# The output projection's pairs and the next pair's attention: from a scheduler's order to one written list of steps

## The chip, the cores and the metric

One Trainium2 chip; the kernel runs on one NeuronCore. Its engines work beside each other, each through its own instructions in order: TensorE (PE: matmuls into PSUM banks of 128 x 512 fp32), VectorE (DVE), ScalarE (ACT), GpSimd (POOL) and SyncE (SP), which issues the DMAs. The metric is device time in microseconds (us) of one execution, the median over runs.

## The reference

Two branches read the layer-normalized `x` (2048 x 1024); the result is `x + s * silu(B)`.

```python
qkv = x @ wqkv                       # 32 heads of 32
phi(p) = concat(softmax(p @ w_phi), softmax(-p @ w_phi))
kv = einsum("bhsf,bhsd->bhfd", phi_k, v);  z = einsum("bhsf->bhf", phi_k)
o  = einsum("bhqf,bhfd->bhqd", phi_q, kv) / (einsum("bhqf,bhf->bhq", phi_q, z)[..., None] + 1e-6)
s  = o.reshape(B, S, D) @ wo
B  = (sigmoid(x @ w_gate) * (x @ w_up)) @ w_down      # F = 3584
out = x + s * silu(B)
```

## The kernel before, in words

Every large product is in fp32 accuracy by splitting: an operand `b` becomes `hi` (rounded by ScalarE, L129) and `lo = b - hi` (VectorE, L130), and `mm3` (L132) makes three matmuls hi·hi, hi·lo, lo·hi (L134 to L136). Every large product is also one level of Strassen's scheme (Winograd's form): of a 2 x 2 blocking seven products, B11, T2, T3, B21, T1, T4, B22 (the numbers 0 to 6), instead of eight, with sums of blocks before and of products behind.

The stages follow each other: projections of q, k, v for the first and the second half of the tokens, the gated GLU for both, the down projection, and last the output projection. The change is in the last one alone, from `NTP = TT // 2` on (L636): the 2048 tokens are 8 pairs of tiles of 128 tokens (`u` = 0, 1), and for every pair the kernel makes the attention's output `o` as operands and multiplies them with `wo`. The weights `wo` lie split in SBUF (`WO`, read by `wo_prep`).

The attention of one pair, `attend(tp_)` (L709), has for each half of the columns (`hb` = 0, 1) two kinds of task:

- `phi_transpose(tp_, u, hb, q)` (L657): four 128 x 128 transposes by TensorE (L662) of the normalized features `e` of tile `u` into one of two PSUM banks (`tpr`), and a split of that bank into `phu` (L129, L130). `e` lies in slot 47 + u and comes from DRAM by `e_load(u)` (L651, 512 KB); after the second task of a tile (`q` = 1) the next `e_load` into the same slot is issued (L668).
- `numerator(tp_, hb, q)` (L671): for `b` = 0, 1 four matmuls of 128 x 256 (L680) into one of two banks (`nmr`); ScalarE copies half the partitions to `oraw` (L684) and VectorE adds the others (L685). Behind the second of a half, `o_operands` (L692) makes Strassen's sums of `oraw` on GpSimd (L697, L700, L701, L705) and splits each of the seven operands into slots of `ofr`.

The output projection of pair `tp_` (L1194 on) runs over the seven products `i` in order 0 to 6; each is four `mm3` over `k`, into a bank of `amm`: B11, T2, T3 and T1 open a bank of their own, B21, T4 and B22 continue those of B11, T3 and T1. Behind each product stands its evacuation: B11 by ScalarE (L1210), T2, T3 and the others by VectorE (L1212, L1214, L1221, L1224), then for the four result blocks a multiplication with the gate `g` and an addition of `x` (L1225, L1226), on GpSimd, or in the last pair for T4 and B22 on VectorE; then the store of the block to `out` (L1227) and `gx_load`, which reads `g` and `x` of the block after the next (L1188, L1189). Between the products' steps the loop takes the 12 tasks of `attend(tp_ + 1)` (L1206): task n when `(13 - len(nxt)) * 3 <= 2 * n`, so the next pair's attention lies between this pair's products. The first pair's attention runs inside the down projection.

What decides the order on each engine: the source is recorded, and the scheduling layer (`schedule_with_timeline_sim=True`, L1254) orders each engine's instructions by its own simulated times. In the built program TensorE runs a middle pair's products as B11, T1, B21, T3, T2, T4, B22, not as the source has them. An exception is the kernel's first stage: a list of named single steps, `FIRST` (L752), that the context manager `in_order` (L906) fixes on PE, DVE, ACT, SP and POOL by chaining every instruction to the one before it on its engine. `queued` holds the last instruction of each.

Of the kernel before, what the change touches and what calls it, by code (L numbers as in the profile page):

```python
# [10 lines left out]
F32 = mybir.dt.float32  # L11
# [7 lines left out]
P = 128  # L19
# [14 lines left out]
class Ring:  # L34
# [3 lines left out]
    def next(self):  # L38
        self.n += 1
        return self.items[(self.n - 1) % len(self.items)]  # L40
# [5 lines left out]
B11, T2, T3, B21, T1, T4, B22 = range(7)  # L46
# [3 lines left out]
def hedgehog_glu_kernel(  # L50
# [11 lines left out]
    nc = tc.nc  # L62
# [53 lines left out]
    def halves(*ids):  # L116
        return [slots[i][:, a] for i in ids for a in range(2)]
# [6 lines left out]
    def pair(i):  # L124
        return slots[i][:, 0], slots[i][:, 1]

    def split(o, src):

        nc.scalar.copy(o[0], src)  # L129
        return nc.vector.tensor_sub(o[1], src, o[0].bitcast(F32))  # L130

    def mm3(o, a, b, first, last, **kw):  # L132

        nc.tensor.matmul(o, a[0], b[0], start=first, stop=False, **kw)  # L134
        nc.tensor.matmul(o, a[0], b[1], start=False, stop=False, **kw)  # L135
        nc.tensor.matmul(o, a[1], b[0], start=False, stop=last, **kw)  # L136
# [5 lines left out]
    side = deque()  # L142
# [163 lines left out]
    opening = (B11, T2, T3, T1)  # L306
# [329 lines left out]
    NTP = TT // 2  # L636
# [3 lines left out]
    phu = Ring((44, 20))  # L640
    ofr = Ring((46, 24, 25, 26, 27, 22, 23, 39, 40, 41, 42))
    res = Ring(halves(49, 52))
    gx = Ring(halves(54, 53))
    tpr, nmr, amm = Ring(banks[:2]), Ring(banks[2:4]), Ring(banks[4:])
    e_next, units_ph, of = [0, 0], {}, {}
    oraw = [slots[50], slots[51]]
# [7 lines left out]
            nc.sync.dma_start(whole(47 + u), e_d[2 * tp_ + u, hb])  # L654
        e_next[u] += 1

    def phi_transpose(tp_, u, hb, q):  # L657
        ps = tpr.next()
        e = whole(47 + u)
        for j in range(4):  # L660
            k = 4 * q + j
            nc.tensor.transpose(ps[:, j * P:(j + 1) * P], e[:, k * P:(k + 1) * P], ident)  # L662
# [4 lines left out]
        split((ph[:, 0, :, cs], ph[:, 1, :, cs]), ps.rearrange("p (k t) -> p k t", t=P))  # L667
        if q:  # L668
            e_load(u)

    def numerator(tp_, hb, q):  # L671

        ph = units_ph[hb, q]
        kg = slots[KVB[hb]][:, q].rearrange("p (k m) -> p k m", m=P)
        for b in range(2):
            ps = nmr.next()
            for j in range(2):
                k = 2 * j + b
                for a in range(2):
                    nc.tensor.matmul(ps[:, j * 256:(j + 1) * 256], kg[:, k], ph[:, a, k], start=a == 0, stop=a == 1)  # L680
            hi, lo = [slice(r * 64, r * 64 + 64) for r in (b, 1 - b)]
            o = oraw[hb][hi].rearrange("p u (g t) -> p g u t", t=P)[:, 2 * q:2 * q + 2]
            y, z = [ps[r].rearrange("p (j u t) -> p j u t", j=2, u=2) for r in (hi, lo)]
            nc.scalar.copy(o, z)  # L684
            nc.vector.tensor_add(o, o, y)  # L685
        if q:
            o_operands(tp_, hb)

    def o_operand(tp_, i, b):
        split(pair(of[tp_][i]), b)  # L690

    def o_operands(tp_, hb):  # L692
        (b11, b12), (b21, b22) = [(o[:, 0], o[:, 1]) for o in oraw]
        if hb == 0:
            of[tp_] = {i: ofr.next() for i in range(7)}
            o_operand(tp_, B11, b11)
            nc.gpsimd.tensor_sub(b11, b12, b11)  # L697
            return
        o_operand(tp_, B22, b22)
        nc.gpsimd.tensor_sub(b12, b22, b12)  # L700
        nc.gpsimd.tensor_sub(b22, b22, b11)  # L701
        o_operand(tp_, T2, b22)
        o_operand(tp_, T3, b12)
        o_operand(tp_, B21, b21)
        nc.gpsimd.tensor_sub(b21, b21, b22)  # L705
        o_operand(tp_, T1, b11)
        o_operand(tp_, T4, b21)

    def attend(tp_):  # L709

        out = []
        for hb in range(2):
            tr = {(u, q): (phi_transpose, tp_, u, hb, q) for u in range(2) for q in range(2)}
            nm = [(numerator, tp_, hb, q) for q in range(2)]

            out += [tr[0, 0], tr[0, 1], tr[1, 0], nm[0], tr[1, 1], nm[1]]
        return out
# [185 lines left out]
    queued = {}  # L903
# [218 lines left out]
    for n, (i, j, cs) in enumerate(dsteps):  # L1122
# [32 lines left out]
            side.extend([lambda u=u: e_load(u) for u in range(2)])  # L1155
        if n == ND - NJ:
            step(1000)
            side.extend([lambda fn=fn, a=a: fn(*a) for fn, *a in attend(0)])
# [15 lines left out]

    done = (B21, T1, T4, B22)
    result = [(tp_, i) for tp_ in range(NTP) for i in done]
    gxs = {}
# [5 lines left out]
    def gx_load():  # L1183
        if result:
            tp_, i = result.pop(0)
            t, cols = rows(tp_, i)
            g, xt = gxs[tp_, i] = gx.next(), gx.next()
            nc.sync.dma_start(g, g_d[t, :, cols])  # L1188
            nc.sync.dma_start(xt, x[t * P:(t + 1) * P, cols])  # L1189

    for _ in range(2):
        gx_load()
    abank = {}
    for tp_ in range(NTP):  # L1194
        nxt = attend(tp_ + 1) if tp_ + 1 < NTP else []
        n = 0
        u1, u2, y11, y21 = [res.next() for _ in range(4)]
        for i in range(7):
            if i in opening:
                abank[i] = amm.next()  # L1200
            ps = abank[{B21: B11, T4: T3, B22: T1}.get(i, i)]
            o = [h.rearrange("p (k t) -> p k t", t=P) for h in pair(of[tp_][i])]
            for k in range(4):
                mm3(ps, (o[0][:, k], o[1][:, k]), pair(WO[i][k]), i in opening and k == 0, k == 3, skip_group_check=True)
                n += 1
                while nxt and (13 - len(nxt)) * 3 <= 2 * n:  # L1206
                    fn, *a = nxt.pop(0)
                    fn(*a)
            if i == B11:
                nc.scalar.copy(u1, ps)  # L1210
            elif i == T2:
                nc.vector.tensor_add(u1, u1, ps)  # L1212
            elif i == T3:
                nc.vector.tensor_add(u2, u1, ps)  # L1214
            else:
                g, xt = gxs.pop((tp_, i))
                t, cols = rows(tp_, i)
                eng = nc.vector if tp_ == NTP - 1 and i in (T4, B22) else nc.gpsimd
                if i == B21:
                    y = y11  # L1220
                    nc.vector.tensor_mul(y, g, ps)  # L1221
                else:
                    y = {T1: u2, T4: y21, B22: u1}[i]
                    nc.vector.tensor_add(y, u2 if i == T1 else u1, ps)  # L1224
                    eng.tensor_mul(y, y, g)  # L1225
                eng.tensor_add(y, y, xt)  # L1226
                nc.sync.dma_start(out[t * P:(t + 1) * P, cols], y)  # L1227
                gx_load()


# [27 lines left out]
```

## Time and profile before

| | |
|---|---|
| median of 3 runs | 2415.2 us (2412.53 to 2416.89) |
| the profiled execution | 2410.82 us, span 2409.0 us |
| PE busy | 2370.0 us, 98% |
| DVE, ACT, POOL busy | 1763.4, 1029.4, 960.4 us |
| DMA | 596.29 MB, mean 248 GB/s |
| granted PE clock, mean | 0.998 |

Busy time of PE counts a matmul's whole pipelined length (390 ns for one of 128 x 512, while the next begins about 0.23 us later), so gaps between matmuls are read from starts and from waits, not from the busy share. The "chain" follows the work that ended last back from the end; a "wait" names the instruction that ended an engine's idle time. `bank<-ident,fc` at L662 are the transposes, `bank<-fb,p` and `bank<-x,p` at L680 the numerators; `fc<-e_d` is an `e_load`, `fc<-g_d` and `fc<-x` a `gx_load`, `out<-fc` (or `fb`, `p`) a store.

### The profile page before, as it was taken

The page shows a single profiled execution, that of the slowest core. Times are in us where ns is not written, and L with a number is a line of the kernel's source. Part 1 is how long each engine was busy: PE and PEld are TensorE (multiplying, and loading weights), DVE is VectorE, ACT ScalarE, POOL GpSimd, SP SyncE. Part 2 cuts the span into 40 slices and gives each one's busy share as a digit, 9 for nine tenths or more (in the row PEclk, how much of TensorE's full clock was granted, in tenths as well). Part 3 has the DMA queues.
Part 4 walks back from the last instruction along what each step waited for, and adds up shares of the span by engine and source line. Part 5 has one row for each costly group of instructions (what it writes and reads, how often), then busy time and mean ns, then how long its engine had stood idle before and what let it go on. Part 6 is the DMA issues. An engine that isn't in the chain of part 4 may idle for free.

```text
span 2409.0 us, 31843 instructions
## 1 busy us (share of the span) xinstructions
PE 2370.0 (98%) x10953; PEld 1967.8 (82%) x10953; DVE 1763.4 (73%) x2323; ACT 1029.4 (43%) x1536; POOL 960.4 (40%) x611
## 2 busy tenths in 40 slices
PE   8999999999999999999999999999999999999998
PEld 7888888888888878788888888888888888878776
DVE  8636777767676689658858888646889988866776
ACT  7334344454544433324434444423443334454443
POOL 1332556656565423122434131323334335414554
PEclk9999999999999999999999999999999999999999
DMA  6788977777686787786877666686676766877554
GB/s 248 246 302 318 360 266 256 269 261 271 238 285 237 259 281 257 246 283 220 278 258 267 205 230 208 211 282 230 216 240 228 227 209 228 284 237 253 186 183 134
DMA packets 232291, 596.29 MB, mean 248 GB/s; under 512 B 30528, under 2 KB 30528, under 8 KB 227520
## 3 DMA queue, kind: packets, MB, share of 16 engines
q1 hardware_dynamic: 232128, 594.25, 71.9%
q8 instruction: 86, 1.41, 0.2%
q14 instruction: 77, 0.63, 0.1%
HBM read 359.01 MB, written 235.14 MB: 247 GB/s over the span
## 4 chain that ended last, share of the span: by engine, by line
PE 83%; DVE 8%; DMA 4%; issue 2%; ACT 2%; POOL 0%; SPq 0%; ACTq 0%; DVEq 0%; POOLq 0%
PE bank L134 27%; PE bank L136 26%; PE bank L135 26%; DVE w L130 2%; PE bank L283 1%; DMA fc<-qkv_d 1%; DMA fc<-xo_d 1%; PE bank L484 1%; PE bank L662 1%; PE bank L680 1%; DVE p L130 1%; DVE x L130 1%; DMA fc<-e_d 1%; PE bank L203 0%; ACT x L129 0%
## 5 line engine op out<-in xcount | busy, mean ns | idle before, releaser
L134 PE MATMUL bank<-x,w 128*128 128x512 f32 x2352 | 911.3, 390 | 6.3 <-ACT fb L1036 2.5
L135 PE MATMUL bank<-x,w 128*128 128x512 f32 x2352 | 915.6, 389 | 0.0
L136 PE MATMUL bank<-x,w 128*128 128x512 f32 x2352 | 907.4, 389 | 0.0
L129 ACT CAST w<-fa 128x512 fp32r<-128x512 f32 (+1 forms) x430 | 293.8, 686 | 550.9 <-PE bank L135 364.4
L134 PEld LDWEIGHTS bank<-x,w 128*128 128x128 f32 x2352 | 441.6, 188 | 100.0 <-ACT fb L1036 3.5
L136 PEld LDWEIGHTS bank<-x,w 128*128 128x128 f32 x2352 | 441.6, 188 | 91.9 <-DVE w L130 0.4
L135 PEld LDWEIGHTS bank<-x,w 128*128 128x128 f32 x2352 | 441.7, 188 | 90.2
L130 DVE TENSOR_TENSOR w<-fa,w 128x512 fp32r<-128x512 f32 (+1 forms) x430 | 415.1, 969 | 106.7 <-ACT w L129 99.8
L136 PE MATMUL bank<-w,x 128*128 128x512 f32 x708 | 277.2, 392 | 4.3 <-DVE x L829 4.3
L134 PE MATMUL bank<-w,x 128*128 128x512 f32 x708 | 278.7, 394 | 0.5 <-DVE fc L414 0.5
L135 PE MATMUL bank<-w,x 128*128 128x512 f32 x708 | 277.0, 391 | 0.0
L1046 POOL TENSOR_TENSOR fb<-fb,fc 128x512 f32<-128x512 f32 x57 | 87.9, 1542 | 240.1 <-DVE fc L1045 237.4
L136 PEld LDWEIGHTS bank<-w,x 128*128 128x128 f32 x708 | 133.3, 188 | 33.6 <-DVE x L829 5.4
L134 PEld LDWEIGHTS bank<-w,x 128*128 128x128 f32 x708 | 133.5, 189 | 27.3 <-ACT w L129 0.9
L135 PEld LDWEIGHTS bank<-w,x 128*128 128x128 f32 x708 | 133.5, 189 | 26.6
L619 POOL TENSOR_TENSOR fc<-fc 128x1024 f32<-128x1024 f32 x32 | 81.7, 2554 | 183.4 <-ACT fc L449 128.4
L1045 DVE TENSOR_TENSOR fc<-fc,bank 128x512 f32<-128x512 f32 x84 | 57.3, 682 | 102.7 <-PE bank L136 93.0
L130 DVE TENSOR_TENSOR x<-fa,x 128x512 fp32r<-128x512 f32 x112 | 115.8, 1034 | 20.2 <-ACT x L129 20.1
L129 ACT CAST w<-fb 128x512 fp32r<-128x512 f32 x112 | 69.3, 619 | 130.9 <-PE bank L135 103.9
L130 DVE TENSOR_TENSOR p<-fc,p 128x1024 fp32r<-128x1024 f32 (+2 forms) x97 | 109.2, 1134 | 11.5 <-ACT p L129 9.5
L129 ACT CAST p<-fc 128x1024 fp32r<-128x1024 f32 (+2 forms) x97 | 70.8, 735 | 105.9 <-DVE fc L465 60.5
L130 DVE TENSOR_TENSOR w<-fb,w 128x512 fp32r<-128x512 f32 x112 | 93.5, 835 | 29.8 <-ACT w L129 25.2
(256 smaller groups left out, 3195.9 us busy)
## 6 DMA issues: line engine op xcount, KB each, us to landing
ws_d<-w SPq DMA_DIRECT2D x112, 512.0 KB, 4.1
w<-ws_d SPq DMA_DIRECT2D x112, 512.0 KB, 5.0
fa<-w_gu SPq DMA_DIRECT2D x84, 512.0 KB, 4.3
fa<-h_d SPq DMA_DIRECT2D x84, 512.0 KB, 4.2
fa<-wf_d SPq DMA_DIRECT2D x32, 1024.0 KB, 6.7
h_d<-fc SPq DMA_DIRECT2D x120, 256.0 KB, 3.6
fc<-e_d SPq DMA_DIRECT2D x48, 512.0 KB, 3.9
fc<-qkv_d SPq DMA_DIRECT2D x80, 256.0 KB, 4.5
```

The costliest lines, as they stand in the source:

```text
L129: nc.scalar.copy(o[0], src)
L130: return nc.vector.tensor_sub(o[1], src, o[0].bitcast(F32))
L134: nc.tensor.matmul(o, a[0], b[0], start=first, stop=False, **kw)
L135: nc.tensor.matmul(o, a[0], b[1], start=False, stop=False, **kw)
L136: nc.tensor.matmul(o, a[1], b[0], start=False, stop=last, **kw)
L283: nc.tensor.matmul(ps[:, gs], r[:, gs], bd[:, 4 * f + g], start=True, stop=True)
L484: nc.tensor.matmul(kvb[g // 2][:, g % 2 * 256:g % 2 * 256 + 256], v[:, g].rearrange("p a f -> p (a f)"), ph[:, g].rearrange("p a f -> p (a ...
L619: nc.gpsimd.tensor_mul(ez, e, zb)
L662: nc.tensor.transpose(ps[:, j * P:(j + 1) * P], e[:, k * P:(k + 1) * P], ident)
L680: nc.tensor.matmul(ps[:, j * 256:(j + 1) * 256], kg[:, k], ph[:, a, k], start=a == 0, stop=a == 1)
L1045: v = nc.vector.tensor_add(b, u2 if q == 3 else u1, bank)
L1046: nc.gpsimd.tensor_mul(g, g, b)
```

## The change

The helpers are cut into single steps: `transposes` and `phi_part` (hi, lo) instead of `phi_transpose`; `numerators` and `numerators_out` (cp, ad) instead of `numerator`; `o_sum` and `o_part` instead of `o_operands`; `products`, `product_out`, `scaled` instead of the body of the last loop. `e_load` follows the second pair of transposes of a tile, in whichever order `q` comes. The first pair's attention, inside the down projection, still runs from `attend`, in the old order. Then one list `PAIR` names the steps of a pair's output projection and of the next pair's attention in one sequence; it is run 8 times, in the last without the attention's steps, and `in_order` fixes it on PE, DVE, ACT and POOL (not on SP).

The names: `tr`, `hi`, `lo` and `u hb q`; `nm`, `cp`, `ad` and `hb q b`; `s11`, `sA`, `sB`, `sC` for GpSimd's sums and `x..h`, `x..l` for the splits; `g` with product and `k` for an `mm3`, `v` for an evacuation, `m` and `a` for the multiplication with the gate and the addition of x. In PAIR the products follow as B11, T2, B21, T3, T1, T4, B22: against the built order before, T2 moves from fifth to second and T1 from second to directly ahead of T4. In the last pair B22 is finished in another way: `vB22` makes g·product (VectorE), GpSimd prepares u1·g + x in `last_rest`, and `aB22` adds both.

```diff
-    gx = Ring(halves(54, 53))
-    def phi_transpose(tp_, u, hb, q):
-        ps = tpr.next()
+    def transposes(u, hb, q):
+        tbank[u, hb, q] = ps = tpr.next()
...
+        taken[u] = taken.get(u, 0) + 1
+        if taken[u] % 2 == 0:
+            e_load(u)
+
+    def phi_part(part, u, hb, q):
...
-        if q:
-            e_load(u)
...
-    abank = {}
-    for tp_ in range(NTP):
-        nxt = attend(tp_ + 1) if tp_ + 1 < NTP else []
...
+    PAIR = """
+        tr100 tr000 hi100 gB110 hi000 lo100 gB111 lo000 gB112 tr001 nm001 hi001 tr101 cp001 lo001 gB113 hi101 nm000
+        lo101 gT20 cp000 vB11 gT21 ad000 gT22 ad001 gT23 gB210 tr010 nm010 hi010 tr110 cp010 lo010 nm011 hi110 ad010
+        gB211 cp011 lo110 tr111 ad011 gB212 hi111 tr011 lo111 gB213 hi011 xB11h nm101 lo011 gT30 cp101 xB11l nm100
+        ad101 s11 gT31 cp100 vB21 gT32 ad100 aB21 nm110 vT2 gT33 cp110 nm111 ad110 gT10 cp111 gT11 ad111 gT12 vT3
+        xB22h sA gT13 xB21h xB22l xT1h gT40 vT1 sB xT3h gT41 xB21l gT42 xT3l sC xT2h gT43 gB220 vT4 mT1 xT4h gB221
+        xT1l gB222 xT2l aT1 gB223 vB22 mT4 xT4l aT4 mB22 aB22""".split()
...
+    def scaled(tp_, i, part):
+        u1, u2, y11, y21 = ys[tp_]
+        g, xt = gxs[tp_, i]
+        y = {B21: y11, T1: u2, T4: y21, B22: u1}[i]
+        last = tp_ == NTP - 1 and i == B22
+        eng = nc.vector if tp_ == NTP - 1 and i in (T4, B22) else nc.gpsimd
+        if part == "m":
+            return last or eng.tensor_mul(y, y, g)
+        eng.tensor_add(y, y, y11 if last else xt)
+        t, cols = rows(tp_, i)
+        nc.sync.dma_start(out[t * P:(t + 1) * P, cols], y)
+        gx_load(result.index((tp_, i)) + 2)
+
+    def last_rest():
+        u1, (g, xt) = ys[NTP - 1][0], gxs[NTP - 1, B22]
+        nc.gpsimd.tensor_mul(u1, u1, g)
+        nc.gpsimd.tensor_add(u1, u1, xt)
...
+    queued.clear()
+    with in_order(*[getattr(mybir.EngineType, e) for e in ("PE", "DVE", "Activation", "Pool")]):
+        for tp_ in range(NTP):
+            ys[tp_] = [res.next() for _ in range(4)]
+            if tp_ + 1 < NTP:
+                of[tp_ + 1] = {i: ofr.next() for i in range(7)}
+            for name in PAIR:
+                ahead, f, found = next((ahead, f, m) for form, ahead, f in pair_forms for m in [re.fullmatch(form, name)] if m)
+                if tp_ + 1 < NTP or not ahead:
+                    f(tp_, *found.groups())
+                if tp_ == NTP - 1 and name == "aT1":
+                    last_rest()
```

More of the change, by code (lines that the diff above doesn't have):

```diff
@@ L709, in attend, with o_sum, o_part @@
-    def attend(tp_):
+    def o_sum(which):
+        (b11, b12), (b21, b22) = [(o[:, 0], o[:, 1]) for o in oraw]
+        o, a, b = {"s11": (b11, b12, b11), "sA": (b12, b22, b12), "sB": (b22, b22, b11), "sC": (b21, b21, b22)}[which]
+        nc.gpsimd.tensor_sub(o, a, b)
+    def o_part(tp_, i, part):
+        (b11, b12), (b21, b22) = [(o[:, 0], o[:, 1]) for o in oraw]
+        b = {B11: b11, T1: b11, B22: b22, T2: b22, T3: b12, B21: b21, T4: b21}[i]
+        hi, lo = pair(of[tp_][i])
+        if part == "h":
+            nc.scalar.copy(hi, b)
+        else:
+            nc.vector.tensor_sub(lo, b, hi.bitcast(F32))
@@ L1193, in hedgehog_glu_kernel @@
-    abank = {}
-    for tp_ in range(NTP):
-        nxt = attend(tp_ + 1) if tp_ + 1 < NTP else []
[L1196 to L1228, printed above, removed]
```

125 lines of the change are left out of this document (84 added, 41 removed).

## The prediction

> **What bounds the kernel now.** I read the page first (span, busy shares, chain), then the chain in order of time over one pair of the last stage, then who TensorE waited for there, and then the queues of GpSimd and SyncE.
>
> ```profile
> span 2409.0 us, 31843 instructions
> ...
> PE 83%; DVE 8%; DMA 4%; issue 2%; ACT 2%; POOL 0%; SPq 0%; ACTq 0%; DVEq 0%; POOLq 0%
> ```
>
> The kernel is bound by TensorE. The built programs have the same instructions in the same order on all engines up to 2177.82 us; only what follows can change. The rows below are from the chain (start, length, what), and then TensorE's waits from 2177.8 on (who for whom: us in total, times, longest).
>
> ```profile
> 2281.16 0.70 DVE fb L1212
> ...
> 2284.57 0.23 PE bank L135
> ...
> 2288.58 0.44 PE bank L662 x4
> 2289.02 0.84 PE bank L680 x7
> ...
> 2296.93 0.59 ACT x L129
> 2297.55 0.69 DVE x L130
> ...
> 2299.00 0.70 DVE fb L130
> ...
> 2310.21 0.70 DVE fc L1212
> ```
>
> ```profile
> PE bank L134 <- DVE fb L1214: 3.0, 4, 1.4
> PE bank L134 <- ACT fa L129: 2.8, 1, 2.8
> PE bank L662 <- DVE x L130: 2.5, 4, 0.6
> PE bank L680 <- DVE fb L130: 1.7, 5, 0.3
> PE bank L662 <- DMA fc<-e_d: 1.0, 2, 0.7
> PE bank L134 <- DVE fc L1214: 0.9, 3, 0.3
> ```
>
> The evacuation of T2's product (L1212) comes back after 2310.21 - 2281.16 = 29.05 us: that is one pair. Its TensorE work at the chain's own prices is 84 matmuls of 0.23, eight groups of four transposes at 0.44 and 32 numerator matmuls at 0.12 (0.84 for seven): 19.3 + 3.5 + 3.8 = 26.7 us. So a pair loses some 2.4 us, and the rows show where: around 2296 to 2299 TensorE has run out of work and waits for ScalarE and VectorE to split a bank of transposes, and at 2281 to 2282 T4's product, which continues T3's bank, waits until T3's sum is read (L1214), and that read stands behind the sum of T2, whose product runs directly ahead. E loads end few waits here (1.0 us in all). In sum this stage has about a dozen microseconds of waits that a better order could take away, 0.5% of the kernel.
>
> **The change, part by part.** *Counts.* TensorE keeps its 10,825 matmuls and SyncE its 1,588 transfers; VectorE has one instruction fewer, GpSimd two more. The price lies in the order alone, and in the four orders that now hold rigidly; SyncE's order is still the scheduler's.
>
> *What goes.* The 2.8 us wait for ACT fa L129 in the last pair, the waits for L1214 (3.9 us; T1's four steps now lie between T3 and T4) and most of the split waits (L662, L680: 4.2 us): in the new list at least one product step stands between most splits and their readers. What is late next is the e transposes of the second half (u = 0, then u = 1, hb = 1: tr010 and tr110). They stand nine product steps into the pair, and their loads can only start when tr001 and tr101 have read the buffers, six steps earlier. I price that below.
>
> *The new loop.* On SyncE in the built order, the pair stores T4's rows, reloads an x, issues the e load of u = 0, then a g load, and only then the e load of u = 1. The store waits for GpSimd's `aT4`, the g load for GpSimd's `mB22`, both of the previous pair. So from one tr110 to the next runs a closed chain:
>
> tr110 → (TensorE in order) nm111 → cp, ad → GpSimd sA, sB, sC, mT1, aT1, mT4, aT4, mB22 → SyncE's g load → e load → tr110.
>
> 1. From tr110 to nm111's end the list has 3 transpose groups, 20 numerator matmuls and 21 product matmuls: 3 x 0.44 + 20 x 0.12 + 21 x 0.23 = 8.5 us. Then the copy and the add, with 0.4 of hand-overs:
>
> ```profile
> L684 ACT COPY fc<-bank 64x512 f32<-64x512 f32 x44 | 25.6, 581 | 44.2 <-PE bank L680 43.4
> ```
>
> ```profile
> L685 DVE TENSOR_TENSOR fc<-fc,bank 64x512 f32<-64x512 f32 x45 | 30.7, 683 | 22.3 <-ACT fc L684 21.6
> ```
>
> 0.58 + 0.68 + 0.4 = 1.7. Together 10.2 us.
>
> 2. GpSimd's groups from 2225 to 2385 us (busy, mean ns | idle before):
>
> ```profile
> L1226 POOL TENSOR_TENSOR fc<-fc 128x512 f32<-128x512 f32 x12 | 16.7, 1392 | 8.5 <-DVE fc L1221 8.0
> L1225 POOL TENSOR_TENSOR fc<-fc 128x512 f32<-128x512 f32 x9 | 14.2, 1581 | 13.0 <-DVE fc L1224 13.0
> L705 POOL TENSOR_TENSOR fc<-fc 128x512 f32<-128x512 f32 x5 | 8.1, 1623 | 0.4
> L701 POOL TENSOR_TENSOR fc<-fc 128x512 f32<-128x512 f32 x5 | 8.1, 1611 | 3.5 <-DVE x L130 2.1 <-DVE fa L130 1.4
> L700 POOL TENSOR_TENSOR fc<-fc 128x512 f32<-128x512 f32 x5 | 6.4, 1282 | 24.5 <-DVE fc L685 24.5
> ```
>
> sA, sB, sC are L700, L701, L705: 1.28 + 1.61 + 1.62. Three multiplications at 1.58 and two additions at 1.39: 7.5. sB and sC each wait for VectorE to have read what they overwrite: 0.7 apiece, L701's idle time a call. 4.5 + 7.5 + 1.4 = 13.4 us.
>
> 3. SyncE: the g load ahead, about 0.4 us between two issues (2322.86 to 2323.30 to 2323.73 below).
>
> 4. The e load itself. The rows: the chain into a transpose, an earlier burst, SyncE's own rows, median times to landing in the stage, and a window with one load alone.
>
> ```profile
> 2234.60 1.26 POOL fb L1225
> ...
> 2235.87 0.32 SPq L1188
> ...
> 2236.25 6.37 DMA fc<-e_d
> ...
> 2242.67 0.44 PE bank L662 x2
> ```
>
> ```profile
> 2207.60 5.76 DMA fc<-e_d
> ```
>
> ```profile
> 2322.86 0.34 SPq L1227 DMA_DIRECT2D out<-fc  x1
> 2323.30 0.38 SPq L1189 DMA_DIRECT2D fc<-x  x1
> 2323.73 4.62 SPq L654 DMA_DIRECT2D fc<-e_d  x2
> ```
>
> ```profile
> fc<-e_d SPq DMA_DIRECT2D x19, 512.0 KB, 4.1
> ...
> out<-fc SPq DMA_DIRECT2D x12, 256.0 KB, 2.5
> ```
>
> ```profile
> fc<-e_d SPq DMA_DIRECT2D x1, 512.0 KB, 3.3
> ```
>
> The first four rows are this very chain, once, in the kernel before: GpSimd's tail, SyncE's g load behind it, an e load that takes 6.37 us among stores and loads, and a transpose that waited. In the new order it is the steady state. Bounds for u = 1's load: 3.3 us (alone) and 6.37 plus what an additional 512 KB just ahead of it costs, under 1.6 (twice 3.3 - 2.5, the price of 256 KB more), so 8.0. It stands directly behind a store, an x, the other e load and a g, so it is nearest to the two burst rows, mean 6.1; the additional 512 KB was issued 0.9 us earlier, so 1.6 - 0.9 = 0.7 of it is felt. I take 6.7 (a burst row of 5.76 + 0.7 = 6.5 to 6.37 + 0.7 = 7.1).
>
> The loop is 10.2 + 13.4 + 0.4 + 6.7 = 30.7 us a pair against 29.05 before and TensorE's 26.7: the pair is then bound by the loop, not by TensorE, and the waits at tr010 and tr110 together come to some 3 us.
>
> *Ends of the stage.* tr110 of the first pair: 27 product matmuls, 5 transpose groups and 12 numerator matmuls after 2177.8, 9.8 us, plus 0.7 for two split waits (the L662 and L680 waits above) and 0.5 for its e load (0 to 1.6): 2188.8. Then six loops. Behind the seventh tr110 stand the rest of that pair (26.7 - 9.8 = 16.9) and the last pair's 84 matmuls (19.3). The tail before:
>
> ```profile
> 2403.35 0.39 PE L136 MATMUL bank<-x,fb 128*128 128x512 f32 x1
> 2403.78 0.69 DVE L1224 TENSOR_TENSOR fb<-fb,bank 128x512 f32<-128x512 f32 x1 [0.58 <-PE bank L136]
> ...
> 2405.23 0.69 DVE L1226 TENSOR_TENSOR fb<-fb,fc 128x512 f32<-128x512 f32 x1
> 2405.95 0.34 SPq L1227 DMA_DIRECT2D out<-fb  x1
> ```
>
> Three VectorE steps of 0.72 before the last store. After: B22 needs two (`vB22`, `aB22`), for which GpSimd prepares u1·g + x; but VectorE's fixed order puts `mT4` and `aT4` between them, and in the last pair both are VectorE's. So four steps, 0.7 later, and GpSimd's two preparing steps end barely in time: 0 to 0.5 more. From the last matmul's end to VectorE's end I count 3.4 us, and the store as before.
>
> **Sum.** VectorE ends at 2188.8 + 6 x 30.7 + 16.9 + 19.3 + 3.4 = 2412.6, before at 2405.23 + 0.69 = 2405.92: 6.7 us later. The chain's prices include a few restarts, so I round down to 6. The profiled execution took 2410.8 (span 2409.0), hence 2417; the median of the runs shown is 2415.2, 4.4 above it, and on that base I predict 2421 us. From no change, 0.2% (4.8 us) is about what a measurement can tell.
>
> **Rivals.** *The loads land in time (faster).* If u = 1's load takes 4.1 us, the stage's median, the loop is 28.1; six pairs save 16 us on the sum above: 2405. It decides at a landing of 5.5 us, where the loop is 29.5 and nothing is gained. For it: that median, and the loads of a lone burst. Against it: both rows with this neighbourhood are above 5.5. The Trainium skill (DMA: Bandwidth & Descriptors, Latency and other measured facts) puts a DMA's fixed cost at about 2 us, mostly the memory's receipt; by that and its fabric rate 512 KB would land in an estimated 3.2 us, and this rival would be the outcome. The lone load agrees, the 6.37 us does not. Chance 0.22.
>
> *They come out even.* At 5.8 us, the nearer burst row with nothing added, the loop is 29.8 and the whole 1 us from before: 2416. Chance 0.2.
>
> *The clock falls.* Two waits of 1.5 us within 3 us may cost TensorE its clock. The stretch of the 2.8 us wait, and the one after it (us, busy by engine, PEclk):
>
> ```profile
> 2384.00:2387.00 3.00, 0.73 (x2) 0.30 (x2) 2.29 (x4) 1.88 (x4) 1.28 (x2) 1.00 0.04 15
> 2387.00:2391.00 4.00, 3.99 (x11) 3.07 (x12) 3.72 (x4) 1.25 (x2) 3.19 (x2) 0.57 0.00 0
> ```
>
> After 3 us with 0.73 of work the clock was 0.57 for 4 us, 1.7 us lost. Four pairs of seven so, inside the loop's TensorE part: 7 us more, 2428. The Trainium skill (TensorE: Matmul & The Clock Gate, The HAM clock gate) says a free-running window of about 3.4 us with too little work halves the clock for the next; the rows agree. With two waits and 0.9 us of work between, it depends on where a window lies. Chance 0.13.
>
> **Numbers.** Forecast 0.45 (2417 to 2425 by the burst rows), clock 0.13, even 0.2, in time 0.22. Faster by over 0.2%: 0.22; within: 0.2; slower: 0.58. Range 2405 to 2428.
>
> **What will show it.** L1245 (T2's evacuation) returns every 30.7 us, not 29.05 or 28. TensorE's longest waits are L663 for DMA fc<-e_d, 1 to 2 us, twice a pair, and L1254's bank waits are gone. The chain of a pair runs GpSimd L701, L1264, L1265, then the e load with 6 to 7 us. The wait for ACT fa and the half clock near 2387 are gone. The last three VectorE rows are L1264, L1265, L1265 after L1251. I am wrong if e loads land within 5.5 us, or if SyncE issues them ahead of GpSimd's last steps.

## The result and the profile after

The changed kernel took 2427.38 us (median of 6 runs, 2422.23 to 2431.3), the kernel before on the same chip 2413.42 (6 runs, 2411.18 to 2416.89). The ratio is 1.0058, with a 95% interval from 1.0047 to 1.0069: 14 us slower. The forecast was 2421 and slower by 6 us, so the sign and the loop came out and the size did not: the median lies above the 2417 to 2425 that went with the forecast, and 0.6 us from the 2428 of the rival "the clock falls". How much of that is the clock is worked out below.

The profiled execution took 2424.19 us. First the return of T2's evacuation, from the groups by form, before and after (`fc` and `fb` take turns by pair; the two numbers behind the durations are the first and the last start).

```profile
L1212 DVE TENSOR_TENSOR fb<-fb,bank x4: 687/689/689, 2222.6 to 2396.4; 128x512 f32<-128x512 f32 x4
```

```profile
L1245 DVE TENSOR_TENSOR fc<-fc,bank x4: 671/672/674, 2197.7 to 2386.8; 128x512 f32<-128x512 f32 x4
```

Six pairs took (2396.4 - 2222.6) / 6 = 28.97 us each before and (2386.8 - 2197.7) / 6 = 31.5 us after. (In kernels with the list I count from the first pair to the seventh; where the scheduler orders, the first pair is longer, and I count from the second to the eighth.) Six pairs at 2.5 us more are 15 us: the loss lies in the pairs' return.

The waits of TensorE from 2177.8 us on (who for whom: us in total, times, longest), after:

```profile
PE bank L663 <- DMA fc<-e_d: 17.3, 12, 2.8
...
PE bank L663 <- DVE fb L677: 3.3, 6, 0.6
```

Before, e loads ended 1.0 us of waits; now 17.3 us. The waits for ACT fa and for the sums (L1214 before, L1247 now) are gone, as is the half clock near 2387. Of the split waits most are still there: 3.3 us for L677 against 4.2 for L130 before. A new wait is larger than all that went.

One turn of the loop, from one tr110 to the next. TensorE's rows for both tr110 (and, between them, its last product matmul and tr010), three of GpSimd's operations (sA, aT4, mB22), SyncE's issues, and the chain's last rows:

```profile
2253.02 1.12 PE L663 MATMUL bank<-ident,fc 128*128 128x128 f32 x4 [0.50 <-DMA fc<-e_d]
...
2279.93 0.39 PE L136 MATMUL bank<-w,x 128*128 128x512 f32 x1
2282.26 0.63 PE L663 MATMUL bank<-ident,fc 128*128 128x128 f32 x4 [1.94 <-DMA fc<-e_d]
...
2284.16 0.66 PE L663 MATMUL bank<-ident,fc 128*128 128x128 f32 x4 [0.80 <-DMA fc<-e_d]
```

```profile
2263.88 1.30 POOL L701 TENSOR_TENSOR fc<-fc 128x512 f32<-128x512 f32 x1 [2.10 <-DVE fc L696]
...
2274.61 1.29 POOL L1265 TENSOR_TENSOR fc<-fc 128x512 f32<-128x512 f32 x1
2275.85 1.30 POOL L1264 TENSOR_TENSOR fc<-fc 128x512 f32<-128x512 f32 x1
```

```profile
2275.93 0.34 SPq L1267 DMA_DIRECT2D out<-fc  x1
2276.32 0.42 SPq L1214 DMA_DIRECT2D fc<-x  x1
2276.84 0.38 SPq L653 DMA_DIRECT2D fc<-e_d  x1
2277.31 0.40 SPq L1213 DMA_DIRECT2D fc<-g_d  x1
2277.76 0.42 SPq L653 DMA_DIRECT2D fc<-e_d  x1
```

```profile
2273.41 0.61 DVE fb L677
...
2274.06 0.66 PE bank L663 x4
...
2275.29 0.44 PE bank L663 x4
...
2277.76 6.35 DMA fc<-e_d
```

From tr110 at 2253.02 to the first sum at 2263.88 are 10.9 us; GpSimd's mB22 ends at 2277.15, 13.3 us after that; SyncE's e load follows 0.6 us later, lands after 6.35, and tr110 starts at 2284.16. That is the closed chain of the prediction, 31.1 us long, with one link that the rows leave open. SyncE issues the store of T4's rows, the x, the e load of u = 0, the g and the e load of u = 1 at 0.39 to 0.52 us from one to the next, and the store starts 0.03 us after `aT4` ends (2275.90). So `aT4` and five issues in a row give the same start for the e load as `mB22` and the g load; which of the two held it isn't shown.

The last fence also shows a second branch that the prediction did not have. tr001 at 2274.06 waits for VectorE's lo000 (L677, in the row above it), and tr101, which frees the e buffer of u = 1, ends at 2275.73. So without GpSimd and SyncE the load could have started at 2275.8 and not at 2277.76: that is only 2 us earlier. In the kernel as built both branches lie close to each other, and behind both stands an e load of over 6 us. TensorE's list has little to do meanwhile: behind tr101 it starts its last product matmul at 2279.93, and tr010 comes at 2282.26.

### The profile page after: what moved, and what is told of

Read it like the earlier page. It is cut to its first block, busy times and chain, and to the rows that moved or that the text cites. A ratio compares the mean times of both kernels' runs of the same rounds, so it can differ in the third digit from the quotient of the medians.

```text
span 2422.4 us, 31803 instructions
## 1 busy us (share of the span) xinstructions
PE 2373.1 (98%) x10953; PEld 1972.6 (81%) x10953; DVE 1771.3 (73%) x2322; ACT 1028.9 (42%) x1536; POOL 957.8 (40%) x613
## 4 chain that ended last, share of the span: by engine, by line
PE 78%; DVE 9%; DMA 6%; issue 3%; ACT 2%; POOL 1%; SPq 1%; DVEq 0%; ACTq 0%; POOLq 0%
PE bank L134 25%; PE bank L135 24%; PE bank L136 24%; DMA fc<-e_d 2%; DVE w L130 2%; PE bank L687 1%; PE bank L283 1%; PE bank L484 1%; PE bank L663 1%; DMA fc<-xo_d 1%; DMA fc<-qkv_d 1%; DVE p L130 1%; DVE x L710 1%; ACT w L129 0%; DVE fa L710 0%
## 5 line engine op out<-in xcount | busy, mean ns | idle before, releaser
L130 DVE TENSOR_TENSOR w<-fa,w 128x512 fp32r<-128x512 f32 (+1 forms) x430 | 418.0, 976 | 106.6 <-ACT w L129 97.8
L130 DVE TENSOR_TENSOR x<-fa,x 128x512 fp32r<-128x512 f32 x112 | 113.5, 1014 | 18.6 <-ACT x L129 18.6
L130 DVE TENSOR_TENSOR p<-fc,p 128x1024 fp32r<-128x1024 f32 (+2 forms) x97 | 107.3, 1114 | 12.0 <-ACT p L129 10.0
L130 DVE TENSOR_TENSOR w<-fb,w 128x512 fp32r<-128x512 f32 x112 | 93.9, 839 | 29.8 <-ACT w L129 25.0
```

## The experiments

All are edits of the changed kernel, except the last. "Pair" is the return of T2's evacuation as above. "Stage" runs from the first transposes of the listed steps to VectorE's end, and so leaves out what differs between executions ahead of it. Both are numbers of one profiled execution; the median is that of all executions. Each ratio is to executions of the kernel before on the same chip, whose medians lie between 2413.05 and 2414.06.

| kernel | median, us | ratio to before, 95% | pair, us | stage, us |
|---|---|---|---|---|
| before | 2413.42 | | 28.97 | 228.1 |
| changed | 2427.38 | 1.0047 to 1.0069 | 31.5 | 239.2 |
| filler | 2426.55 | 1.0038 to 1.0072 | 31.0 | 238.7 |
| t1_bare | 2415.88 | 1.0001 to 1.0020 | 30.0 | 229.2 |
| e_on_act | 2410.23 | 0.9975 to 0.9996 | 28.9 | 225.1 |
| halves | 2409.15 | 0.9971 to 0.9990 | 28.7 | 222.5 |
| halves_act | 2409.78 | 0.9979 to 0.9999 | 28.9 | 224.7 |
| act_nogx | 2403.45 | 0.9943 to 0.9969 | 27.9 | 217.2 |
| pool_free | 2422.71 | 1.0022 to 1.0053 | 31.1 | 236.7 |
| pe_only | 2421.78 | 1.0023 to 1.0049 | 30.2 | 236.9 |
| pe_free | 2463.56 | 1.0179 to 1.0213 | 37.3 | 279.0 |
| recorded | 2403.11 | 0.9947 to 0.9975 | 27.5 | 218.9 |
| rec_halves | 2400.64 | 0.9925 to 0.9955 | 26.8 | 212.7 |
| before_halves | 2412.60 | 0.9983 to 1.0009 | 28.9 | 226.4 |

The questions came in three steps. First: is it the loop, and which link? My theories were that the e loads are issued late behind GpSimd's work on SyncE (the late issue), that they land slowly among other transfers (the burst), and that the waits cost TensorE its clock. Then: how much is the landing by itself? And last: is it the sequence of steps that is at fault, or that four engines may not leave it?

**e_on_act.** The e loads of the listed steps are issued from ScalarE's queue and so stand behind no store and no g load.

```diff
-            nc.sync.dma_start(whole(47 + u), e_d[2 * tp_ + u, hb])
+            (nc.scalar if listed else nc.sync).dma_start(whole(47 + u), e_d[2 * tp_ + u, hb])
```

> The e loads of the listed steps are issued from ScalarE's queue, right behind the transposes that free the buffer; nothing else moves. Theory L (the closed loop through SyncE: the loads leave late, behind a store and a g load that wait for GpSimd): in the changed kernel the load of u = 0 leaves 2.0 us and that of u = 1 about 1.8 us later than its buffer is free; issued at once they also stand ahead of that pair's store, x and g in the DMA engines. The load wait of TensorE (17.3 us in all) falls below 4 us, a pair takes 27.5 to 28.3 us, no half clock, and the whole 2404 to 2409 us. Rival B (the distance of six product steps is too short for a load among so many transfers, wherever it is issued): the load still takes 5 us or more, a pair stays above 29.5 us and the whole above 2414.

17 us less than the changed kernel, and the pair 28.9: between the two theories' numbers. The chain of this kernel at the same place:

```profile
2270.59 0.61 DVE fb L677
2271.25 0.66 PE bank L663 x4
...
2272.48 0.45 PE bank L663 x4
2272.95 6.75 DMA fc<-e_d
2279.74 0.66 PE bank L663 x4
```

The load now starts 0.02 us after the transposes that free its buffer, and lands no sooner: 6.75 us. By the means of the six turns from tr110 to tr110, the way from GpSimd's first sum to the issue fell from 14.0 to 11.9 us. Of the 2.6 us a pair the earlier issue is thus worth 2.1; TensorE's part of the turn is 0.7 shorter, as this stage has no half clock (the next experiment is about that), and the landing 0.3 longer (6.8 for 6.5). The rest of the loop stands: VectorE's lo000, tr001, tr101, the load, tr110. Transfers to landing from 2200 to 2375 us, first of the changed kernel, then of this one (KB each, median us):

```profile
fc<-g_d SPq DMA_DIRECT2D x23, 256.0 KB, 2.8
fc<-x SPq DMA_DIRECT2D x23, 256.0 KB, 3.7
```

```profile
fc<-g_d SPq DMA_DIRECT2D x25, 256.0 KB, 5.1
fc<-x SPq DMA_DIRECT2D x24, 256.0 KB, 6.1
```

The second queue brought no faster path: the loads of g and x, which now share the time with the e loads, take nearly twice as long, and so do most of the stores (`out<-fc` 5.9 us for 2.5, `out<-p` 4.6 for 2.4; `out<-fb` 4.0 in both). The Trainium skill (DMA: Bandwidth & Descriptors, Issuing engines are not separate DMA queues) says that transfers from whatever engine run on the same 16 DMA engines and interleave, and that issuing from several saves only the time of the issue; these rows agree.

**filler.** 28 more transposes of `ident` ahead of tr010 and tr110, into the bank that they overwrite anyway, so that TensorE is busy while it waits.

```diff
+        if listed and (hb, q) == (1, 0):
+            for n in range((20, 8)[u]):
+                nc.tensor.transpose(ps[:, n % 4 * P:(n % 4 + 1) * P], ident, ident)
```

> TensorE gets 20 transposes of the identity ahead of the first, and 8 ahead of the second transposes that wait for an e load (into the bank that they overwrite, so the result is the same). The waits stay, but TensorE is busy in them. Theory C (the half clock of four windows is a part of the loss by itself): no window of half clock in the stage, every pair at 30.5 us as the undisturbed ones of the changed kernel, against 31.65, 31.60, 30.52, 32.96, 31.86, 30.55; 6 us less, 2421 us, and runs closer together. If the clock is only along for the ride (the loop waits for the load anyway): within 1.5 us of the changed kernel, 2426 to 2429.

The stage's stretch, changed and filler (length, busy time of five engines, then PEclk, DMA share, GB/s):

```profile
2177.80:2425.00 247.20, 217.19 (x1131) 181.99 (x1129) 166.30 (x218) 100.02 (x174) 121.25 (x87) 0.96 0.53 177
```

```profile
2177.80:2425.00 247.20, 236.11 (x1345) 201.91 (x1343) 170.25 (x221) 101.46 (x177) 124.56 (x89) 1.00 0.56 184
```

The clock is full again, the pair 0.5 us shorter, and the time is the same. That does not clear the clock, as the terms of the turn show. In the changed kernel TensorE ran at half clock in four windows of 3.41 us, each behind the wait at tr010; this stretch is one of them (the third number from the end is PEclk):

```profile
2315.78:2319.20 3.42, 3.42 (x16) 3.02 (x15) 1.85 (x3) 1.16 (x2) 0.00 (x0) 0.50 0.06 20
```

These windows lie in the loop's own TensorE part, from tr110 to nm111. In the turn shown above that part took 10.86 us with copy and add (2253.02 to 2263.88). The same turn with the fillers, tr110 and the first sum:

```profile
2259.06 0.66 PE L666 MATMUL bank<-ident,fc 128*128 128x128 f32 x4 [0.66 <-DMA fc<-e_d]
```

```profile
2269.30 1.30 POOL L704 TENSOR_TENSOR fc<-fc 128x512 f32<-128x512 f32 x1 [2.09 <-DVE fc L699]
```

10.24 us, and 10.20 to 10.24 in all six turns. In the changed kernel it is 10.24 in the two turns without a half clock, and 11.56, 10.86, 11.84 and 11.04 in the four with one: 0.7 us a turn on the mean, 4.4 us in all. The fillers took that away and gave it back: in the first pair, whose loads land early, they hold tr110 up by 2.4 us (12.85 us behind the first transposes, and not 10.43), and u = 1's loads took 0.2 us longer to land. So the half clock is a part of the loss, and these fillers are no repair. The profiled execution with the fillers also reached the stage 4.1 us later (2184.08 and not 2179.95), which is not theirs.

Which waits cost the clock can be read, too. The four windows start 30.72, 64.85 and 30.72 us apart, which is 9, 19 and 9 times 3.413 us. The two stretches of that grid ahead of tr110 in pairs 3 and 7 (the first number behind the length is PE's busy time):

```profile
2247.51:2250.92 3.41, 1.37 (x8) 0.86 (x7) 0.00 (x0) 0.00 (x0) 0.00 (x0) 1.00 0.97 296
```

```profile
2373.79:2377.21 3.42, 1.83 (x9) 1.18 (x7) 0.45 (x1) 0.00 (x0) 0.05 (x1) 1.00 0.88 264
```

Behind the first, half clock; behind the second, none. The other three half windows of the stage follow stretches with 1.34, 1.36 and 0.86 us of busy time, and in pairs 4 and 7, where the waits lie otherwise on the grid, no stretch has less than 1.83.

**t1_bare.** GpSimd's multiplication and addition for T1's block are left out.

```diff
-            return last or eng.tensor_mul(y, y, g)
-        eng.tensor_add(y, y, y11 if last else xt)
+            return last or i == T1 or eng.tensor_mul(y, y, g)
+        if i != T1:
+            eng.tensor_add(y, y, y11 if last else xt)
```

> Leaves out GpSimd's two steps of block T1 (the multiplication with the gate and the addition of x: T1's rows are stored without them). No transfer is left out or added. Theory L, GpSimd's link: its chain from sA to mB22 loses two steps of 1.4 to 1.6 us, SyncE's store and g load leave up to 3 us earlier, and so do the e loads, until they are bound by their buffers (2 us): a pair takes 28.5 to 29.5 us, 12 to 18 us less than the changed kernel, 2409 to 2415 us. Rival B: GpSimd is off the path, the waits for e loads stay as they are, 2425 to 2429 us.

11.5 us less, 0.9 above the range expected: GpSimd is a link, as said. But two operations of 1.6 to 1.7 us are gone from each turn and the pair fell by 1.5 us, not by 3.3. Half of the 1.5 is TensorE's part, 10.2 us again, as no half clock fell into this stage; the way from the first sum to the e load's issue is only 0.8 us shorter. The load of u = 0 now leaves 0.2 us after tr001, so the second branch holds it, and that branch does not pass through these operations; the load of u = 1 still leaves 1.1 us or more after tr101.

**halves.** Each e load is cut into two halves of 256 KB, and each half is issued after the transposes that read it.

```diff
-            nc.sync.dma_start(whole(47 + u), e_d[2 * tp_ + u, hb])
+            nc.sync.dma_start(slots[47 + u][:, q], e_d[2 * tp_ + u, hb, :, q * HB:(q + 1) * HB])
...
-        taken[u] = taken.get(u, 0) + 1
-        if taken[u] % 2 == 0:
-            e_load(u)
+        e_load(u, q)
```

> Each e load is issued in two halves of 256 KB (one per transposes task), the half that the next transposes need first as soon as its part of the buffer is read, three product steps earlier; all on SyncE as before. Rival B (too short a distance): 2.1 us more for each first half, so the load waits fall by some 2 us a pair, 2412 to 2416 us. Theory L: on SyncE the first halves stand behind the same waits for GpSimd, so little is gained: a pair of 29.5 to 30.5 us, 2418 to 2425 us.

It gained more than either theory allowed. A half for tr010 and tr110 is free after tr000 and tr100, before the branches above have closed, so it shortens the issue and the landing alike; the expectation had put the halves behind SyncE's same queue. What remains is 28.7 us a pair, and the wait has moved to the second half of u = 1: the chain has DVE L675 (lo000), tr001, tr101 to 2273.48, SyncE's e half and g load, and at 2275.64 an e half of 6.18 us. VectorE's branch and SyncE's row of issues both stand in it.

**halves_act.** Halves, ScalarE's queue, and in PAIR `mT4` and `aT4` ahead of `vB22`.

```diff
-        xT1l gB222 xT2l aT1 gB223 vB22 mT4 xT4l aT4 mB22 aB22""".split()
+        xT1l gB222 xT2l aT1 gB223 mT4 aT4 vB22 xT4l mB22 aB22""".split()
```

> Both edits that each took 11 to 18 us off: the e loads in halves, each issued from ScalarE's queue right behind the transposes that free it; and in the last pair VectorE runs mT4 and aT4 ahead of vB22. If the late issue and the short distance are two shares of one wait (the load is needed before it lands), together they end it: no wait of TensorE for e loads over 0.5 us, 27.2 to 27.8 us a pair (28.7 with halves alone, 28.9 with ScalarE's queue alone), and what is left is the split wait of 0.5 us a pair: 2400 to 2404 us, clearly faster than the kernel before. If the transfers themselves are the bound (some 2.3 MB a pair and bursts of 1.5 MB), the two don't add: 28.5 us and 2407 to 2410. The tail: VectorE's end 2.6 us behind the start of the last matmul, as in the kernel before, against 4.0 us in the changed kernel.

No better than halves alone. TensorE's waits for e loads did fall, from 7.4 to 2.6 us in all, but those for the splits (L675) rose from 3.2 to 6.8: with the loads out of the way VectorE's list is what TensorE waits for. (A pair moves more than the 2.3 MB named above: in the changed kernel 29.25 MB in 175 us, or 5.3 MB in a pair's 31.5 us.) The tail did get shorter, though not to the 2.6 us expected: from the last matmul's start to VectorE's end 2394.80 to 2398.51, 3.7 us, against 2402.02 to 2406.36, 4.3, in halves.

**act_nogx.** e_on_act, with the g and x loads left out after the first two blocks.

```diff
+        if n < 2:
             nc.sync.dma_start(g, g_d[t, :, cols])
             nc.sync.dma_start(xt, x[t * P:(t + 1) * P, cols])
```

> The kernel with e loads on ScalarE's queue, and g and x loaded for the first two blocks only (30 blocks take what stands in the buffers, so their numbers are not the reference's): 60 loads of 256 KB less, the stores stay. If the neighbours make the e load of u = 1 slow (6.8 us at the head of a pair with ScalarE's queue, 3.3 alone): 4.5 us or less there, no waits for loads but the first pair's, 27.5 us a pair, 2400 us. If the e loads slow each other (two of 512 KB within 1.0 us): still 6 us, 28.5 us a pair or more.

With half a megabyte less to read per block, e loads land in 4.4 us at the median and not 5.4, and the pair falls from 28.9 to 27.9. The loop goes by u = 1's load alone: it took 5.8 us on the mean of the six turns, against 6.8 with g and x, so these transfers are worth 1 us a pair. The larger part of what stands above the 3.3 us of a load alone stays with little else than the load of u = 0, issued 1.0 us ahead; that one landed in 3.4 to 3.5 us in the middle turns. The pair is still above TensorE's 26.7 us of work.

**recorded.** The same steps are recorded in the same sequence, but nothing fixes them; the scheduling layer orders each engine by its own simulated times.

```diff
-    with in_order(*[getattr(mybir.EngineType, e) for e in ("PE", "DVE", "Activation", "Pool")]):
+    if True:
```

> The changed kernel's steps and their sequence, but the engines' orders left to the scheduling layer (in_order is not applied to the pairs). If the loss lies in the rigid orders (a step that waits holds up what stands behind it: GpSimd's last steps, and through SyncE the e loads), the scheduler spreads them again: 28.0 to 29.1 us a pair in the middle, 2402 to 2413 us. If it lies in the sequence itself (the transposes of the second half of the columns nine product steps into the pair), it stays above 30 us a pair and 2420.

2403.11: 24 us below the changed kernel and 0.4% below the kernel before. With the same e loads of 512 KB from the same queue, TensorE isn't once seen waiting for one: in the built order the transposes are spread over the pair's product matmuls, and the loads are issued apart from each other and land in 3.2 to 6.1 us. Which of the two does it was not tried. So the single steps in their new sequence are worth something; the fixed orders cost more than that.

**pool_free, pe_only and pe_free.** Which of the four orders is it? In the first GpSimd alone is set free, in the second only TensorE is held, in the third TensorE alone is set free.

```diff
-    with in_order(*[getattr(mybir.EngineType, e) for e in ("PE", "DVE", "Activation", "Pool")]):
+    with in_order(*[getattr(mybir.EngineType, e) for e in ("PE", "DVE", "Activation")]):
```

> The changed kernel, with GpSimd no longer held to its listed order; TensorE, VectorE and ScalarE keep theirs. The scheduler then puts two e loads ahead of a store that they stood behind, since GpSimd interleaves its sums with the scalings. Theory G (what costs is the loop through GpSimd's fixed list and SyncE to the e loads): the pair falls from 31.5 us to at most 29 us and the time is 2403 to 2412. Theory P (what costs is TensorE's fixed list, which can't step past a transpose whose e load is late, whatever makes it late): the pair stays at 30.5 us or more and the time is 2418 or more.

> The changed kernel, with only TensorE held to its listed order; VectorE, ScalarE and GpSimd are ordered by the scheduler. Theory G: as with GpSimd alone set free, 2403 to 2412, and within 3 us of that run. Theory P: TensorE's list is unchanged, so 2418 or more. A third reading, that the lists of VectorE and ScalarE hold it back: at least 4 us below the run with GpSimd alone set free.

> The changed kernel, with TensorE ordered by the scheduler and VectorE, ScalarE and GpSimd held to their lists. Theory G: GpSimd's list still closes the loop, so the e loads stay late and the time stays between 2417 and 2430. Theory P: TensorE puts products of the pair in front of the transposes, the waits for e loads disappear, and the time is 2400 to 2410, near the 2403.1 of the kernel without any listed order.

Setting GpSimd free gave almost nothing, which theory G did not allow. GpSimd now takes scalings between its sums, and VectorE's splits come later for it: tr001 starts 11.3 us after the first sum and not 10.2. The chain of pool_free, then GpSimd and SyncE in the same turn:

```profile
2245.06 0.61 DVE fb L677
...
2246.94 0.44 PE bank L663 x4
...
2248.61 6.59 DMA fc<-e_d
```

```profile
2246.15 1.28 POOL L1265 TENSOR_TENSOR p<-p,fc 128x512 f32<-128x512 f32 x1
```

```profile
2247.46 0.34 SPq L1267 DMA_DIRECT2D out<-p  x1
```

The two branches now end together (tr101 at 2247.38, GpSimd's addition at 2247.43), and the load of u = 1 still leaves 1.2 us later, behind the store that follows the addition and an x. From the first sum to its issue are 13.9 us on the mean of the six turns, for 14.0 in the changed kernel: this edit did not take the load out from behind GpSimd and SyncE. Neither did pe_only, with three engines free. Its chain:

```profile
2303.70 1.25 POOL p L1265
2304.97 0.34 SPq L1267
2305.36 0.42 SPq L1214
2305.84 6.68 DMA fc<-e_d
```

This is the closed chain of the prediction again, 30.2 us a pair. So the time that theory P gave (2418 or more) came in both runs, but they don't decide between P and G: the load stayed late in both, and e_on_act, with TensorE's list kept, has a pair of 28.9 us. In pe_free theory P fails outright: TensorE free beside three fixed lists is the slowest kernel of all. The scheduler put the transposes of both halves close together, and SyncE's four e loads of a pair in a row behind GpSimd's last step; two landings lie in one turn, as its chain shows:

```profile
2265.45 6.53 DMA fc<-e_d
...
2278.98 4.68 DMA fc<-e_d
```

So no single list is shown to be "the" culprit: neither GpSimd nor TensorE set free alone, nor TensorE held alone, came near the 2403 us of orders that were all computed together. Which engines must be free together for that was not tried.

**rec_halves and before_halves.** The scheduled steps of recorded with the halves; and the halves in the kernel before.

> Two edits together: the steps of the changed kernel ordered by the scheduler (2403.1 by itself) and each e load cut in two halves of 256 KB, each issued after the transposes that free it (2409.2 by itself). Theory L (late e loads are what is left in the scheduled kernel too): below 2400. Theory S (without the fixed lists TensorE steps past a late load, so an earlier load buys nothing): 2401 to 2407. More DMA issues could also cost something: 2408 or more would say that.

> The kernel before (its own interleave, ordered by the scheduler), with each e load cut in two halves of 256 KB, each issued after the transposes that free it. Theory S (before waits for its operand splits on ScalarE and not for e loads, so earlier loads buy it nothing, and what the scheduled steps with halves gain, 2400.6, comes from splitting the operations into single steps): 2411 to 2417, the pair stays near 29.05 us. Theory L (earlier e loads let the scheduler bring the operand splits forward in this kernel too): 2398 to 2406, so the single steps would be worth nothing.

rec_halves is the fastest, 2400.64 us, ratio 0.994 (0.9925 to 0.9955). Its median lies between the two expectations (below 2400, 2401 to 2407), and its runs (2398.84 to 2402.38) touch those of recorded (2402.33 to 2408.66), so the times alone hardly tell the two apart. Its pairs are shorter, though:

```profile
L1243 DVE TENSOR_TENSOR fb<-fb,bank x4: 686/686/689, 2222.0 to 2382.9; 128x512 f32<-128x512 f32 x4
```

(2382.9 - 2222.0) / 6 = 26.8 us, against 27.5 in recorded: that is about TensorE's work in a pair, 26.7 us. In the kernel before the halves change nothing (interval 0.9983 to 1.0009), as it did not wait for e loads. The gain of 0.6% thus needs the single steps in their new sequence (the two were not tried apart), an order that isn't fixed, and for its last part the halves.

## Why the prediction was right and where it was off

*Right: the loop.* Its four terms as predicted and as measured in the turn above: TensorE's part with copy and add 10.2, measured 10.9 (the turn has a half-clock window in it); GpSimd 13.4, measured 13.3; SyncE 0.4, measured 0.6; landing 6.7, measured 6.35. Sum 30.7 predicted, 31.1 measured, mean of six turns 31.5. The rows that should show it did: L1245's return, L663's waits for `fc<-e_d` twice a pair, the order of SyncE's issues. Whether `mB22` or SyncE's row of issues holds the last e load is open, as said.

*Off: the size, 14 us for 6.* VectorE ended at 2419.16 and not at 2412.6. The terms of the sum, by the rows above and below: the first transposes of the stage, before and after; a stretch ahead of the stage, before and after (PEclk is the third number from the end); the seventh tr110; the tail.

```profile
2177.82 1.03 PE L662 MATMUL bank<-ident,fc 128*128 128x128 f32 x8
```

```profile
2179.95 1.03 PE L663 MATMUL bank<-ident,fc 128*128 128x128 f32 x8
```

```profile
2124.63:2128.04 3.41, 3.41 (x17) 2.81 (x16) 1.96 (x4) 1.53 (x3) 0.00 (x0) 1.00 0.50 148
```

```profile
2124.63:2128.04 3.41, 3.41 (x9) 2.62 (x8) 1.65 (x3) 1.54 (x3) 0.00 (x0) 0.50 0.42 128
```

```profile
2379.52 0.66 PE L663 MATMUL bank<-ident,fc 128*128 128x128 f32 x4 [1.02 <-DMA fc<-e_d]
```

```profile
2415.12 0.39 PE L136 MATMUL bank<-x,fb 128*128 128x512 f32 x1
...
2415.60 0.69 DVE L1251 TENSOR_TENSOR p<-fc,bank 128x512 f32<-128x512 f32 x1 [2.09 <-PE bank L136]
2416.20 0.68 DVE L1264 TENSOR_TENSOR p<-p,fc 128x512 f32<-128x512 f32 x1
2416.65 1.36 POOL L1273 TENSOR_TENSOR fb<-fb,fc 128x512 f32<-128x512 f32 x1 [0.43 <-DMA fc<-x]
2416.92 1.63 DVE L1265 TENSOR_TENSOR p<-p,fc 128x512 f32<-128x512 f32 x1
2418.48 0.68 DVE L1265 TENSOR_TENSOR fb<-fb,p 128x512 f32<-128x512 f32 x1
```

- The stage began at 2179.95, not 2177.82: +2.1. This is not the change's. The program ahead of it is the same; in this execution the clock was halved for 3.41 us at 2124.63, in the one before it was not. In the other profiles of this document it begins anywhere from 2173.9 (halves_act) to 2184.1 (filler).
- The first tr110 came 10.4 us later, at 2190.38, not 11.0: -0.55. The 27 product matmuls are there as counted; the two split waits are not.
- Six loops: (2379.52 - 2190.38) / 6 = 31.52, not 30.7: +4.9. By the means of the six turns TensorE's part took 10.96 us, not 10.2; GpSimd and SyncE together 14.0, not 13.8; landing and hand-over 6.5, not 6.7. So the term that was mis-sized is the loop's TensorE part, and what lengthened it is the half clock: 0.7 us a turn, 4.4 us in all (filler). At full clock it is the 10.2 us of the sum. The forecast had the clock at nothing and left it to a rival.
- From the seventh tr110 to the last matmul's end 2415.12 + 0.39 - 2379.52 = 36.0, not 36.2: -0.2.
- The tail 2418.48 + 0.68 - 2415.51 = 3.65, not 3.4: +0.25. It has the four VectorE steps that were named; one of them took 1.63 us and not 0.68, as GpSimd's preparing step ran beside it to 2418.01.

Together +6.6, the difference found. From its first transposes to VectorE's end the stage took 239.2 us, against 228.1 before: 11.1 us longer, where the sum had 6.7. I also rounded 6.7 down to 6, for nothing. The medians are 14.0 us apart; what the other 3 us are, one profile of each kernel can't tell. The six executions of the changed kernel go with their mean granted clock: 2422.2 us at 0.996, 2424.2 and 2425.9 at 0.994, 2428.9 twice at 0.993, 2431.3 at 0.992. (The count of matmuls in the prediction is off without effect: both pages have 10,953.)

*Missed: the second branch.* The prediction had one closed chain. VectorE's list closes a second, 2 us shorter, through lo000 and tr001. It changed no number of the forecast, but it limits what a repair is worth: taking the load out from behind GpSimd and SyncE gave 2.1 us a pair (e_on_act), about the distance between the branches, and leaving out two of GpSimd's operations, 3.3 us, gave 0.8 (t1_bare).

*The rivals.* "Loads land in time" and "come out even" needed a landing of 4.1 or 5.8 us; it was 6.35 here, and 5.81 to 7.17 in the other five pairs' loads of u = 1. The rule of about 2 us of fixed cost, from which 3.2 us followed (the Trainium skill, DMA: Bandwidth & Descriptors, Latency and other measured facts), does not hold for the loads that close the loop; the measurement decides: even in act_nogx, with fewer neighbours, they took 5.8 on the mean. "The clock falls" came true as to the mechanism, with half clock in four pairs of seven, inside the loop's TensorE part as it said, and was too dear: priced at 7 us, worth 4.4 in the profile's six turns. That the median comes within 0.6 us of its 2428 is in part chance: its 7 us were 2.6 too many, and of the 14.0 us between the medians only 11.1 are found in the two profiles of the stage.

## What to carry to other kernels

When an order is written out by hand and fixed on several engines, draw for every buffer the ring "last reader, next load's issue, landing, first reader", with the landing as it is among the neighbours the transfer will really have, and see how much work the list puts between last and first reader; here it was about 4.4 us, from tr101's end at 2275.73 to 0.23 us after the last product matmul's start at 2279.93, for a load of over 6. Look for all the branches that close such a ring before pricing a repair, since removing the longest gains no more than the distance to the next. A wait on an engine whose clock falls with idleness, here TensorE, can also cost more than itself, when the half clock behind it lies in the same ring: price it as a term of the ring. And record the finer steps first without fixing them: here that alone was 0.4% faster than before, where the fixed lists were 0.6% slower.

## What the runs showed that I had not expected

Loads moved to another engine's queue started 2 us earlier and took as long, and the other transfers' time to landing nearly doubled (g 2.8 to 5.1 us, x 3.7 to 6.1). The half clock came in windows on a grid of 3.413 us; in the changed kernel's profile, from 2177.8 us to the last matmul, it came behind stretches of that grid with 1.37 us of TensorE work or less and behind none with 1.83 or more, and its four windows cost 4.4 us. And a VectorE operation between SBUF operands beside a GpSimd one ended 0.54 us after it (1.63 us instead of 0.68, above): the Trainium skill (SBUF — State Buffer, SBUF: two separate sides) calls the port that the two share an exclusive lock, the later one blocked for the whole instruction; the end of this row agrees with an operation that got the port only when GpSimd's was over.
